# Rows of w_out in runs of four, and every fourth column of w_in as weights

## The chip, the cores and the metric

The kernel runs on one core of one Trainium2 chip. The core has five engines that run side by side: TensorE (matmuls; its weight loads are listed apart), VectorE, ScalarE, GpSimd and SyncE, called PE, PEld, DVE, ACT, POOL and SP in the profile. Transfers between the chip's main memory and the on-chip memory are issued by SP, ACT or POOL and carried by 16 DMA engines that all of them share. The metric is the device time of one execution in microseconds (us), lower is better, given as the median of several runs.

## What is computed

Two layers are fused. The first is attention with a sliding window of 128 tokens and a bias that falls off linearly with distance, over 8 batches, 8 heads, 576 tokens and 64 columns a head. The second is a dense layer pair with a hard-swish between: its input is the attention's output, taken as 4608 tokens of 512 columns. Cut to what matters:

```python
# q, k, v: (8, 8, 576, 64); w_in: (512, 2048); w_out: (2048, 512)
scores = q @ k.T / sqrt(64) - slope[head] * abs(i - j)     # kept where 0 <= i - j < 128
attn = softmax(scores) @ v
x = attn.transpose(0, 2, 1, 3).reshape(4608, 512)
h = x @ w_in
g = h * clip(h + 3, 0, 6) / 6
out = g @ w_out
```

The column of `h` that a row of `w_out` is multiplied with has the same index, from 0 to 2047. How the 2048 indices are divided among partitions and tiles is free, as long as both weights do it alike.

## The kernel before

Tokens are worked through in tiles. The attention of a batch is done head pair by head pair (32 pairs in all, `g` in the code), and its output is transposed into `xT`, a ring of 2304 tokens (`RING`, line 50) with the 512 model columns on the partitions in four slices. The dense pair goes over nine tiles of 512 tokens (`NT`).

For a token tile, `moe_up` (line 462) makes 16 blocks of 128 columns of `h`. Block `ms` takes four matmuls (`up_mms`, line 444), one for each slice `ks` of the model columns: the weights are a 128x128 piece of `w_in_sb`, the moving operand is 512 columns of `xT`. The fifth token tile reaches past the end of the ring, and there each matmul is cut into two of 256 columns, each with a weight load of its own (lines 445 to 449). ScalarE takes a clipped form of the block out of the accumulator (line 470) and VectorE multiplies it with the block itself, to bf16 in `gbuf` (line 471): partition `p` of block `ms` holds one column of `h` for all 512 tokens.

`moe_down` (line 488) takes 128 tokens at a time and accumulates 16 matmuls, one for each `ms`, whose weights are a piece of `gbuf` and whose moving operand is `w_out_sb[:, ms, :]`, 512 columns (line 501). The sums are copied out (line 510) and stored. The last 128 tokens have a routine of their own (`last_rows`, line 474).

The order of the work is written out by hand, for every engine and queue (`manual_schedule`, line 716). The strings in `ORDER` (line 513) interleave up blocks (U) and quarters of down steps (D), and `fill` (line 523) puts them between the steps of attention. An engine carries out its instructions in the order in which the code issues them.

The weights come in through POOL's queue, since these transfers turn float32 into bf16 on their way. `load_w_in(g)` (line 164) loads 512 columns of `w_in`. `load_w_out(g)` (line 169) loads 512 rows of `w_out` into four blocks of `w_out_sb`: row `g*512 + m*128 + p` goes to partition `p`, block `4*g + m`, so each row of 512 values is a run of its own. The four calls stand in `second_batch` (line 632), after POOL's casts of v of batch 1 and ahead of its mask for head pair 7 (line 354, written to `gbuf`) and its casts of k and q of batch 2 (line 227). Ahead of this time `w_out_sb` serves as room for the attention of batch 0 (`rooms`, line 281), so that matmuls of lines 383 and 391 also read it.

On SP's queue, `load_tokens(2, "v")` (lines 108 to 113, five transfers of rows of 256 bytes) follows at line 639, behind a small POOL write at line 638, then the k and q loads of batch 3 (lines 98 and 112). POOL casts v of batch 2 into `vbuf` (lines 187 and 190) and the matmuls of attention (lines 383 and 391) read that.

Of the kernel before, what the change touches and what calls it, by code (L numbers as in the profile page):

```python
# [18 lines left out]
def kernel(  # L19
# [9 lines left out]
    nc = tc.nc  # L29
# [23 lines left out]
    xT = perm.tile([128, n_ks, RING + SP - S], BF16)  # L53
    w_in_sb = perm.tile([128, n_ks, d_ff], BF16)
    w_out_sb = perm.tile([128, n_ms, d_model], BF16)
    ident = perm.tile([128, 128], BF16)
    bias3 = perm.tile([128, 1], FP32)
    warm = perm.tile([128, 1], FP32)
# [111 lines left out]
    def load_w_out(g):  # L170
        nc.gpsimd.dma_start(  # L171
            out=w_out_sb[:, ts(g, 4), :],
            in_=moe_w_out[ds(g * 512, 512), :].rearrange("(m p) d -> p m d", p=128))

    def second_w_in():
        nc.gpsimd.memset(w_out_sb[:, 4, 0:1], 0.0)
# [267 lines left out]
    def up_mms(nt, ms, k0, k1, hps):  # L444
        at0 = nt * NT % RING
        n = min(NT, RING - at0)
        for lo, hi, src in ((0, n, at0), (n, NT, 0)):
            if lo == hi:
                continue
            for ks in range(k0, k1):  # L450
                nc.tensor.matmul(hps[:, lo:hi], lhsT=w_in_sb[:, ks, ts(ms, 128)],  # L451
                                 rhs=xT[:, ks, ds(src, hi - lo)],
                                 start=(ks == 0), stop=(ks == n_ks - 1))

    def up_begin(nt, ms, n):
        hps = ps_h.tile([128, NT], FP32, tag="h", name="hps")
        up_mms(nt, ms, 0, n, hps)
        begun[nt, ms] = hps, n
# [3 lines left out]
    def moe_up(nt, ms):  # L462
        gts[nt] = gbuf[nt % 2]
        hps, n = begun.pop((nt, ms), (None, 0))
        if hps is None:
            tag = UP_BANKS.get(ms, "h") if nt == 0 else "h"
            hps = BANKS[tag].tile([128, NT], FP32, tag=tag, name="hps")
        up_mms(nt, ms, n, n_ks, hps)
        r6 = rpool.tile([128, NT], FP32, tag="r6", name="r6")
        nc.scalar.activation(out=r6, in_=hps, func=ACT.Relu, bias=bias3[:, 0:1], scale=1.0 / 6.0)  # L470
        nc.vector.scalar_tensor_tensor(out=gts[nt][:, ms, :], in0=r6, scalar=1.0, in1=hps,  # L471
                                       op0=ALU.min, op1=ALU.mult)
# [145 lines left out]
    def second_batch():  # L618
# [12 lines left out]
        for i in range(4):  # L631
            load_w_out(i)
# [131 lines left out]
```

## Time and profile before

| what | value |
|---|---|
| median of 3 runs | 322.76 us (322.67 to 324.89) |
| profiled execution | 323.3 us, of which the span is 321.6 us |
| granted TensorE clock | 0.998 |
| up matmuls, line 451 | 640 of them, 144.8 us busy |
| down matmuls, line 501 | 560 of them, 137.8 us busy |
| w_out transfers, line 171 | 4 of 512 KB, 7.9 to 15.6 us from issue to landing |
| w_in transfers, line 166 | 4 of 512 KB, 6.3 to 9.5 us from issue to landing |

The span runs from the first to the last instruction of one profiled execution. A line of a group gives the code line, the engine, the operation, what it writes and reads, how many there are; then their busy time in us, the mean length of one in ns, and the idle time of the engine just before them with what ended it. A line of the chain or the timeline gives the start in us, the length in us, and what ran. A line of a stretch gives its length and then, for each engine, its busy time in the order PE, PEld, DVE, ACT, POOL, followed by the clock, the share of the DMA engines and the GB/s. Records of matmuls and of weight loads overlap, so the length of one record is longer than the pace at which they follow one another.

### The profile page before, as it was taken

The numbers are of one execution on the slowest core, as the hardware profiler recorded it, in microseconds if no ns is written. First come the engines' busy times: TensorE is split into PE (matmuls) and PEld (weight loads), VectorE is DVE, ScalarE is ACT, GpSimd is POOL, SyncE is SP. The second block draws the span as 40 slices with busy tenths as digits, with TensorE's granted clock in tenths as the row PEclk, the third lists the DMA queues.
The fourth block names the chain that finished last, engine by engine and source line by source line (L and its number), as shares of the span: only waits on it lengthen the run. The fifth ranks groups of instructions, "written<-read, shape, count | busy, mean of one in ns | idle before, by whom it ended". The sixth has DMA issues, their size and how long they took to land.

```text
span 321.6 us, 7050 instructions
## 1 busy us (share of the span) xinstructions
PE 312.4 (97%) x2738; PEld 167.6 (52%) x2738; DVE 173.0 (54%) x338; ACT 195.6 (61%) x334; POOL 141.1 (44%) x249
## 2 busy tenths in 40 slices
PE   7889999999999999999999999999999999999996
PEld 5565465455555554554667654554554444444443
DVE  6667674554456555555555555555655455455510
ACT  3758976877767766766676667666764344244401
POOL 8455493594493767366745665463331000000000
PEclk9999999999999999999999999999999999999999
DMA  7999999899999999999999989922112200000112
GB/s 276 202 333 208 247 270 196 210 258 194 212 248 166 244 201 203 193 229 199 192 199 202 237 173 212 214 72 86 23 53 66 75 34 35 33 33 33 67 53 77
DMA packets 131425, 51.90 MB, mean 161 GB/s; under 512 B 118976, under 2 KB 123328, under 8 KB 131392
## 3 DMA queue, kind: packets, MB, share of 16 engines
q1 hardware_dynamic: 126160, 45.36, 66.2%
q0 software_dynamic: 4224, 4.19, 8.2%
q10 hardware_dynamic: 1008, 1.90, 1.6%
q8 instruction: 21, 0.34, 0.5%
q14 instruction: 12, 0.10, 0.1%
HBM read 36.70 MB, written 9.44 MB: 143 GB/s over the span
## 4 chain that ended last, share of the span: by engine, by line
PE 82%; DMA 10%; SPq 2%; POOL 2%; DVE 1%; ACT 1%; issue 1%; POOLq 0%
PE ops L501 37%; PE hps L451 33%; DMA w_out_sb<-in_moe_w_out_dram 5%; DMA ldbuf<-in_v_dram 3%; PE scd L296 3%; DMA ldbuf<-in_k_dram 2%; PE av L391 2%; SPq L112 2%; PE av L383 2%; PE sco L328 1%; PE ops L482 1%; PE w L153 1%; POOL w_out_sb L171 1%; PE tp L219 0%; ACT kTb L244 0%
## 5 line engine op out<-in xcount | busy, mean ns | idle before, releaser
L471 DVE SCALAR_TENSOR_TENSOR gbuf<-r,hps 128x512 bf16<-128x512 f32 x144 | 98.7, 687 | 102.5 <-ACT r L470 100.2
L470 ACT ACTIVATE r<-hps,bias 128x512 f32<-128x512 f32 x144 | 98.9, 689 | 88.9 <-PE hps L451 88.7
L451 PE MATMUL hps<-xT,w_in_sb 128*128 128x512 bf16 (+1 forms) x640 | 144.8, 358 | 0.5 <-ACT xT L438 0.3
L501 PE MATMUL ops<-w_out_sb,gbuf 128*128 128x512 bf16 x560 | 137.8, 379 | 0.3 <-DMA w_out_sb<-in_moe_w_out_dram 0.3
L451 PEld LDWEIGHTS <-w_in_sb 128*128 128x128 bf16 x640 | 59.2, 98 | 54.8 <-issue 0.8
L501 PEld LDWEIGHTS <-gbuf 128*128 128x128 bf16 x560 | 51.8, 98 | 56.7 <-issue 0.6
L354 POOL TENSOR_SCALAR_AFFINE_SELECT pd<-pd 128x512 bf16<-128x512 bf16 x48 | 29.7, 634 | 34.5 <-ACT pd L351 34.5
L364 POOL TENSOR_SCALAR_AFFINE_SELECT po<-po 128x512 bf16<-128x512 bf16 x48 | 30.3, 636 | 32.5 <-ACT po L361 32.3
L351 ACT ACTIVATE pd<-scd,bias_d 128x512 bf16<-128x512 f32 x48 | 31.7, 685 | 4.7 <-PE scd L296 4.7
L510 DVE COPY osb<-ops 128x512 f32<-128x512 f32 x33 | 22.7, 687 | 20.4 <-PE ops L501 20.2
L361 ACT ACTIVATE po<-sco,bias_o 128x512 bf16<-128x512 f32 x48 | 33.0, 688 | 0.0
L194 POOL CAST tbuf<-ldbuf 128x512 bf16<-128x512 f32 (+1 forms) x45 | 25.6, 614 | 16.7 <-DMA qTb<-tbuf 9.0
L402 DVE TENSOR_TENSOR avs<-av,rc 128x384 bf16<-128x384 f32 (+1 forms) x48 | 23.6, 491 | 1.6
L391 PEld LDWEIGHTS <-pd 128*128 128x128 bf16 x192 | 14.3, 97 | 8.3 <-issue 0.5
L383 PE MATMUL av<-vbuf,po 128*128 128x65 bf16 x192 | 18.0, 193 | 0.0
L391 PE MATMUL av<-vbuf,pd 128*128 128x65 bf16 x192 | 17.3, 194 | 0.3 <-ACT kTb L244 0.3
L187 POOL CAST vbuf<-ldbuf 128x1024 bf16<-128x1024 f32 x14 | 14.3, 1044 | 4.3 <-DMA ldbuf<-in_v_dram 4.3
L383 PEld LDWEIGHTS <-po 128*128 128x128 bf16 x192 | 14.3, 98 | 2.9 <-DVE avs L402 0.5
L367 ACT ACTIVATE p4buf<-sco,bias_d 128x64 bf16<-128x64 f32 x48 | 15.5, 324 | 0.0
L227 POOL CAST pr<-ldbuf 128x576 bf16<-128x576 f32 x20 | 12.9, 670 | 5.0 <-DMA ldbuf<-in_k_dram 3.1
L296 PE MATMUL scd<-qTb,kTb 64*128 64x128 bf16 x256 | 12.7, 219 | 1.7 <-DVE kTb L220 0.9
L296 PEld LDWEIGHTS <-kTb 64*128 64x128 bf16 x256 | 7.2, 94 | 13.4 <-issue 9.7
(96 smaller groups left out, 217.4 us busy)
## 6 DMA issues: line engine op xcount, KB each, us to landing
out_dram<-osb SPq DMA_DIRECT2D x33, 256.0 KB, 2.4
ldbuf<-in_v_dram SPq DMA_DIRECT2D x32, 256.0 KB, 5.6
ldbuf<-in_q_dram SPq DMA_DIRECT2D x20, 256.0 KB, 4.9
ldbuf<-in_k_dram SPq DMA_DIRECT2D x16, 256.0 KB, 4.5
ldbuf<-in_q_dram SPq DMA_DIRECT2D x12, 288.0 KB, 7.3
ldbuf<-in_k_dram SPq DMA_DIRECT2D x12, 288.0 KB, 7.6
w_in_sb<-in_moe_w_in_dram POOLq DMA_DIRECT2D x4, 512.0 KB, 8.8
w_out_sb<-in_moe_w_out_dram POOLq DMA_DIRECT2D x4, 512.0 KB, 11.6
```

Source lines behind the costliest of these rows:

```text
L194: nc.gpsimd.tensor_copy(out=tbuf[:m, :, j, :], in_=s[:m, j, :, :].rearrange("p (i e) d -> p i (e d)", e=2))
L296: nc.tensor.matmul(scd[:, e, ts(j, 128)], lhsT=kT[r, j, :], rhs=qT[r, j, :], start=first, stop=first or j == 3)
L351: nc.scalar.activation(out=pd[:, e, :, :].rearrange("p j c -> p (j c)"), in_=sc[:, e, :], func=ACT.Exp, bias=bias_d[:, h:h + 1], scale=scale)
L354: nc.gpsimd.affine_select(out=pd[:, e, :, :], in_=pd[:, e, :, :], pattern=[[0, 4], [1, 128]], channel_multiplier=-1, base=0, compare_op=AL ...
L361: nc.scalar.activation(out=po[:, e, :, :].rearrange("p j c -> p (j c)"), in_=sc[:, e, :], func=ACT.Exp, bias=bias_o[:, h:h + 1], scale=scale)
L364: nc.gpsimd.affine_select(out=po[:, e, :, :], in_=po[:, e, :, :], pattern=[[0, 4], [-1, 128]], channel_multiplier=1, base=-1, compare_op=A ...
L383: nc.tensor.matmul(out_av, lhsT=po[:, e, qt % 4, :], rhs=vb[:, qt - 1, h, :], start=True, stop=False)
L391: nc.tensor.matmul(out_av, lhsT=d, rhs=vb[:, qt, h, :], start=(qt == 0), stop=True)
L451: nc.tensor.matmul(hps[:, lo:hi], lhsT=w_in_sb[:, ks, ts(ms, 128)], rhs=xT[:, ks, ds(src, hi - lo)], start=(ks == 0), stop=(ks == n_ks - 1))
L470: nc.scalar.activation(out=r6, in_=hps, func=ACT.Relu, bias=bias3[:, 0:1], scale=1.0 / 6.0)
L471: nc.vector.scalar_tensor_tensor(out=gts[nt][:, ms, :], in0=r6, scalar=1.0, in1=hps, op0=ALU.min, op1=ALU.mult)
L501: nc.tensor.matmul(ops[nt, sub], lhsT=gts[nt][:, ms, ts(sub, 128)], rhs=w_out_sb[:, ms, :], start=(ms == 0), stop=(ms == n_ms - 1))
```

## The change

The w_out transfer takes its 512 rows in another order. Row `g*512 + p*4 + m` now goes to partition `p`, block `4*g + m`: a partition gets four neighbouring rows, 8 KB of float32 in one run, into 4 KB of its own that also lie together. To match, block `ms` of the up step must hold the columns `(ms // 4)*512 + 4*p + ms % 4` of `h`. A view of `w_in_sb` with the columns divided by four gives them: the weights of an up matmul are 128 columns that lie four apart, 8 bytes in bf16. The loads of w_in, the number and order of all instructions, and the down matmuls are as before.

```diff
@@ -53,6 +53,7 @@
     w_in_sb = perm.tile([128, n_ks, d_ff], BF16)
     w_out_sb = perm.tile([128, n_ms, d_model], BF16)
+    w_in_cols = w_in_sb.rearrange("p k (g c m) -> p k g m c", g=4, m=4)
@@ -170,7 +171,7 @@
     def load_w_out(g):
         nc.gpsimd.dma_start(
             out=w_out_sb[:, ts(g, 4), :],
-            in_=moe_w_out[ds(g * 512, 512), :].rearrange("(m p) d -> p m d", p=128))
+            in_=moe_w_out[ds(g * 512, 512), :].rearrange("(p m) d -> p m d", p=128))
@@ -448,7 +449,7 @@
             for ks in range(k0, k1):
-                nc.tensor.matmul(hps[:, lo:hi], lhsT=w_in_sb[:, ks, ts(ms, 128)],
+                nc.tensor.matmul(hps[:, lo:hi], lhsT=w_in_cols[:, ks, ms // 4, ms % 4, :],
                                  rhs=xT[:, ks, ds(src, hi - lo)],
                                  start=(ks == 0), stop=(ks == n_ks - 1))
```

## The prediction

> **What bounds the kernel now.** I read the page first (busy shares, then the chain that ended last, then the costliest groups), then the waits of TensorE, then the stretch from 41 to 60 us, in which w_out is loaded, and last the pace of single matmuls in the timeline and the chain.
>
> ```profile
> span 321.6 us, 7050 instructions
> PE 312.4 (97%) x2738; PEld 167.6 (52%) x2738; DVE 173.0 (54%) x338; ACT 195.6 (61%) x334; POOL 141.1 (44%) x249
> ...
> PE 82%; DMA 10%; SPq 2%; POOL 2%; DVE 1%; ACT 1%; issue 1%; POOLq 0%
> ...
> L451 PE MATMUL hps<-xT,w_in_sb 128*128 128x512 bf16 (+1 forms) x640 | 144.8, 358 | 0.5 <-ACT xT L438 0.3
> ...
> L451 PEld LDWEIGHTS <-w_in_sb 128*128 128x128 bf16 x640 | 59.2, 98 | 54.8 <-issue 0.8
> ```
>
> TensorE is the bound: it works in 312.4 of 321.6 us. The chain's "DMA 10%" is misleading. A chain passes through whatever released a step, however short the wait was. Half of that 10% is the w_out transfer, and the next three answers (the chain, TensorE's waits, the busy time of the stretch) show what it really costs:
>
> ```profile
> 43.46 15.55 DMA w_out_sb<-in_moe_w_out_dram
> 59.05 1.02 PE ops L501 x4
> ...
> PE ops L501 <- DMA w_out_sb<-in_moe_w_out_dram: 0.3, 1, 0.3
> ...
> 41.00:60.00 19.00, 18.05 (x193) 10.49 (x191) 11.22 (x20) 14.65 (x25) 11.26 (x19) 1.00 1.09 214
> ```
>
> The last quarter of w_out lands 15.55 us after its issue, but TensorE waits for it only once, for 0.33 us (the timeline has the matmuls of line 501 at 59.05 with 0.33 us of idle before them). In the whole stretch TensorE is idle for 19.00 - 18.05 = 0.95 us.
>
> Whether the other half of the change costs anything depends on how long one weight load may take before a matmul waits for it. The chain gives the pace of matmuls that follow one another, each with its own weight load:
>
> ```profile
> 156.80 0.03 PE av L383
> 156.83 0.03 PE av L391
> 156.86 0.03 PE av L383
> 156.89 0.03 PE av L391
> 156.92 1.75 PE hps L451 x16
> 158.66 0.86 PE ops L501 x4
> ```
>
> A matmul with 512 columns takes 0.86/4 = 216 ns. One with 256 columns takes 1.75/16 = 109 ns. The narrow ones of attention (65 columns) follow one another every 30 ns, and each of them loads 128x128 weights of its own. So a contiguous load occupies the load path for at most 30 ns, although its record shows 98 ns: the records overlap.
>
> **The change, part by part.** The sum is made against the profiled execution, 323.3 us, of which 321.6 us are span and 1.7 us lie around it. It stands 0.5 us above the median, 322.76 us.
>
> *1. The four w_out transfers have other rows.* Nothing is moved: four issues at the same places in POOL's order and the same bytes. In the DMA packet records each load is now 512 packets, 32 for each of 16 engines, of 1024 B written (2048 B read); four neighbouring rows make 128 packets, 8 an engine, of 8192 B read. The records give a packet's price by its size. Beside 22 ns for 256 B (between 40 and 60 us) stand 108 ns for 2304 B, thus some 11 ns plus 0.042 ns a byte, and w_out's own packets fit at 96 ns undisturbed. A packet of 8192 B would take 11 + 344 = 355 ns in place of 4 x 96 = 384, so an engine is done with its 32 rows 32 x 29 = 0.9 us sooner. While v of batch 2 shares the engines (52 to 55 us), the records alternate one to one (154 packets of w_out and 155 of v in a us), so fewer, larger packets also give w_out more of each engine. From below the gain is nothing, if the packets are cut as before. From above it is 0.33 us, since TensorE waits no longer than that; with a knock-on it cannot pass the 0.95 us of idle in the stretch. I take 0.33 us, because 0.9 us sooner is more than that. The first three quarters land ahead of their use already: issue to landing takes 7.9 us at the least against a first use 10.5 us after the issue (41.23 to 51.71), and TensorE shows no other wait for them.
>
> *2. The loads behind it.* What w_out gains in share, v of batch 2 on SP's queue loses while both are under way. SP issues that load from 47.95 to 59.90 us, one issue of it taking 6.29 us, and the k and q loads of batch 3 follow on the same queue. Up to 56 us v got 750 of its 4608 packets; afterwards it moves 985 in a us. Held back entirely, it would have 750/985 = 0.8 us more to move after w_out, which is 0.9 us earlier: as much as before. The reader behind it is POOL's cast (line 187, done at 63.6 us, which waits for v for 0.6 us), and behind that the matmuls of attention at 64.53 us. They have 0.9 us in hand, so 0 is the price, and at most 0.8 us would be lost if w_out were no quicker and that reserve were gone.
>
> *3. POOL's issues.* Each takes 0.76 us (3.0 us for four). With a quarter of the runs it may be shorter; SP's issues differ little by runs (0.53 us for 128 of 2304 B, 0.70 for 1024 of 256 B). So it is between no change and 3.0 us less. What stands behind on POOL is the mask on gbuf at 44.20 to 45.46 us, read by the matmuls at 47.02 us. With 1.5 us in hand there is nothing to gain: 0.
>
> *4. The weights of line 451 are every fourth column, 8 bytes apart.* There are 640 loads, 512 under matmuls of 216 ns and 128 under matmuls of 109 ns (the token tile that wraps round the ring). If such a load occupies the path for L ns, the cost is 512 x (L - 216) + 128 x (L - 109), each counted only where it is above zero. No row shows a strided weight load, so I bound it. From below: 30 ns as now, costing 0; no gain is possible, since the loads are covered already. The nearest rate on TensorE itself is that of the moving operand, one column at a time: 128 columns in 216/4 = 54 ns, costing 0. At half that rate it is 107 ns, costing 0 by a hair. At a quarter it is 214 ns: 128 x 105 = 13.4 us. From above, four times the whole record: 4 x 98 = 392 ns, or 512 x 176 + 128 x 283 = 126 us. I take 0, by the two nearest things in the trace. One is the 54 ns, at which TensorE is seen to take in columns one after another from the same memory. The other is far, ScalarE reading with a long step:
>
> ```profile
> 46.93 0.63 ACT L438 COPY xT<-tb 128x576 bf16<-128x576 bf16 x1
> 47.45 0.77 ACT L244 COPY kTb<-tp 128x640 bf16<-128x640 bf16 x1
> ```
>
> The first reads its columns in order, the second every 128th column: 1.09 and 1.20 ns an element, so the step costs a tenth and not a factor. The cover of 216 and 109 ns is 3.6 times the present load even in the tight form.
>
> [...]
>
> Sum: 323.3 - 0.33 + 0 + 0 + 0 = 323.0 us for the profiled execution, and 322.76 - 0.33 = **322.4 us** for the median.
>
> **The rivals.**
> *Slower: strided weights no longer fit under the matmul.* Place: line 451. It decides from L = 109 ns, first in the tile with matmuls of 256 columns, and is worth 1% (3.2 us) from L = 134 ns. At a quarter of the streaming rate, 214 ns, the time is 322.8 + 13.4 = 336.2 us. Above 216 ns every up matmul waits, and 392 ns would give 322.8 + 126 = 449 us. For it: no row shows such a load, and TensorE has 3% of idle in all, so anything uncovered shows in full. Against it: the cover, 3.6 and 7 times the present load. Also against it: the 128 weights are spread over four times the bytes, and if the load had to pass over them all at its present pace it would take 4 x 30 = 120 ns, which costs 128 x 11 = 1.4 us and gives 324.2 us, still within 1%.
> *No effect: w_out comes no sooner, or the wait returns.* Either the packets are cut as before, or the slowest engine still sets the landing. For it: the records of completion for the last load run from 55.6 to 57.3 us for fifteen engines and to 58.7 us for one, so one late engine holds back the whole. Time: 322.8 us.
> *Faster by more than 1%.* That needs 3.2 us; the stretch in which the transfer matters has 0.95 us of idle, so 321.8 us is the floor of this mechanism. Only a wait elsewhere that moves by chance could do more.
>
> **How the numbers follow.** The smallest difference that a measurement of this kernel can tell from no change is about 1%. The forecast (loads covered, 0.33 us gained) has 0.52; no effect 0.19; pitch between 109 and 216 ns 0.13, of which 0.03 stays under 1%; pitch above 216 ns 0.14; faster by over 1% 0.02. So within 1% is 0.52 + 0.19 + 0.03 = 0.74, slower 0.10 + 0.14 = 0.24, faster 0.02. The range reaches from 321.6 us (the floor of 321.8, less the spread of 0.1 us between median and lowest run) to 336.2 us (a quarter of the rate). It leaves out 0.14 + 0.02 = 0.16. The likeliest case's own range is 321.6 to 323.5 us.
>
> **What would show it.** The L451 weight loads should still last about 98 ns, or up to twice that, with the up matmuls at 216 and 109 ns. The software queue should have some 1500 packets fewer (4 x 384), the last w_out transfer should land before 58.7 us, and TensorE's wait for it should be gone. POOL's cast of v should end by 64.5 us. I am wrong if the chain shows L451 at more than 0.86 us for four, if TensorE's busy time grows, or if a wait for v appears ahead of the matmuls at 64.5 us.

## The result and the profile after

The changed kernel takes 344.06 us (median of 4 runs, 341.66 to 347.94) against 323.07 us before (median of 4): a ratio of 1.0613, with a 95% interval of 1.0539 to 1.0687. It is 6% slower. The ratio compares the means of the faster executions, without the one of 347.94 us. Its profiled execution took 341.66 us, with a span of 340.0 us, 18.4 us more than the profiled execution before. The forecast of 322.4 us and the whole range missed it.

The page of the changed kernel, beside the one of before (the code lines have moved by one, so line 451 is now 452 and 501 is 502):

```profile
span 340.0 us, 7011 instructions
PE 311.8 (92%) x2699; PEld 178.3 (52%) x2738; DVE 173.7 (51%) x338; ACT 196.0 (58%) x334; POOL 139.8 (41%) x249
...
PE   7853199999999999999999999999999999999996
...
PEclk9997589999999999999999999999999999999999
...
L452 PE MATMUL hps<-xT,w_in_sb 128*128 128x512 bf16 (+1 forms) x623 | 144.6, 361 | 17.2 <-DMA w_in_sb<-in_moe_w_in_dram 16.0
```

TensorE's busy time is about what it was, 311.8 us against 312.4 (some matmul records are missing from this trace, 2699 of 2738, so it reads a little low). So the matmuls did not become slower by anything like 18 us, and there is no sign of weight loads that hold them up. What grew is idle time, and nearly all of it lies in three slices of the PE row, between 17 and 43 us. The group of up matmuls says what ended it: a transfer of **w_in**, which the change does not touch. TensorE's waits say how much (us in total, times, the longest), and the timeline of its weight loads (start in us, length, operation, idle before it) shows the place:

```profile
PE hps L452 <- DMA w_in_sb<-in_moe_w_in_dram: 16.0, 2, 10.5
```

```profile
22.27 0.11 PEld L452 LDWEIGHTS <-w_in_sb 128*128 128x128 bf16 x1
27.97 0.14 PEld L452 LDWEIGHTS <-w_in_sb 128*128 128x128 bf16 x2 [5.59 <-DMA w_in_sb<-in_moe_w_in_dram]
...
30.20 0.15 PEld L452 LDWEIGHTS <-w_in_sb 128*128 128x128 bf16 x1
41.38 0.14 PEld L452 LDWEIGHTS <-w_in_sb 128*128 128x128 bf16 x2 [11.03 <-issue]
```

The first block of the first token tile loads its weights for slice 0 of the model columns at 22.27 us, as early as before. Its second load, slice 1, waits until 27.97 us: until the second w_in transfer has landed, whose columns it does not read. The second block does the same. Slice 0 goes at 30.20 us, and slice 1 waits until 41.38 us, when the third and fourth transfers are in. Before the change these loads followed one another without a gap:

```profile
21.94 0.37 PEld L451 LDWEIGHTS <-w_in_sb 128*128 128x128 bf16 x3
```

The waiting goes the other way as well. In the code the third and fourth w_in loads (lines 607 and 608 of the kernel before) stand behind three matmuls of the first block (line 603) and ahead of the second block's (line 612). This fits that it is the second block that waits for them. And POOL now holds these two loads back until the three matmuls are done, though they write none of the columns that those read. Before, and after the change (in brackets the idle time of POOL and what ended it):

```profile
27.83 1.48 POOL L166 DMA_DIRECT2D w_in_sb<-in_moe_w_in_dram  x2
```

```profile
29.32 1.48 POOL L167 DMA_DIRECT2D w_in_sb<-in_moe_w_in_dram  x2 [2.23 <-PE hps L452]
```

So the transfers for which the second block waits also start 1.5 us later.

From this the 18.4 us can be added up. From the first up load to the first down matmul it was 51.71 - 21.94 = 29.8 us and is 70.5 - 22.27 = 48.2 us, 18.4 us more. From there to the end of the span it was 269.9 us and is 269.5. So the whole loss lies ahead of the first down matmul: 16.0 us are the two waits, and 2.4 us are left. The row PEclk points to those. The granted clock falls to 0.7 and 0.5 in the last two idle slices; its mean is 0.76 from 20 to 41 us and 0.91 from 41 to 60 us. By finer stretches it is 1.00 from 22.3 to 27.2 us, 0.50 from 27.4 to 30.7, 1.00 from 30.8 to 34.1, 0.50 from 34.3 to 44.3 and 1.00 from 44.5 to 60. TensorE's timeline shows what the matmuls after each wait then take, and the chain, in the last two lines, has the landing that ends the second wait and nine transposes at the full clock:

```profile
27.98 1.04 PE L452 MATMUL hps<-xT,w_in_sb 128*128 128x512 bf16 x2 [5.49 <-DMA w_in_sb<-in_moe_w_in_dram]
28.82 0.74 PE L433 MATMUL tb<-ident,avs 128*128 128x128 bf16 x5
29.35 1.17 PE L255 MATMUL tp<-ident,pr 128*128 128x128 bf16 x9
30.31 0.59 PE L452 MATMUL hps<-xT,w_in_sb 128*128 128x512 bf16 x1
41.41 1.44 PE L452 MATMUL hps<-xT,w_in_sb 128*128 128x512 bf16 x3 [10.51 <-DMA w_in_sb<-in_moe_w_in_dram]
42.64 1.16 PE L255 MATMUL tp<-ident,pr 128*128 128x128 bf16 x9
43.60 1.64 PE L452 MATMUL hps<-xT,w_in_sb 128*128 128x512 bf16 x5
45.07 0.67 PE L255 MATMUL tp<-ident,pr 128*128 128x128 bf16 x9
...
30.05 11.22 DMA w_in_sb<-in_moe_w_in_dram
...
45.24 0.50 PE tp L255 x9
```

The starts give the pace. From 27.98 to 30.31 us run two up matmuls and fourteen transposes, 2.33 us, where 216 ns for an up matmul and 0.50/9 = 56 ns for a transpose would make 1.2. From 41.41 to 45.07 us run eight up matmuls and nine transposes, 3.66 us in place of 2.2. Together that is 2.5 us more, about what was left. What ran slowly between the two waits cost little by itself, since TensorE would otherwise have waited there longer; the 1.4 us behind the second wait could not be hidden. The stretches agree with this: the clock stands at half from some 5 us into the first wait of 5.5 us, again from some 3.3 us into the second of 10.5 us, and in full from about 3 us after the second. What sets the clock is not shown here. The median of the runs lies further off, 21.0 us above. The waits differ from execution to execution (17.6 us in the profiles of two experiments below), which may be why.

### The profile page after: what moved, and what is told of

Same layout as the page of the kernel before. It is cut to its first block, busy times and chain, and to the rows that moved or that the text cites. A ratio compares the mean times of both kernels' runs of the same rounds, so it can differ in the third digit from the quotient of the medians.

```text
span 340.0 us, 7011 instructions
## 1 busy us (share of the span) xinstructions
PE 311.8 (92%) x2699; PEld 178.3 (52%) x2738; DVE 173.7 (51%) x338; ACT 196.0 (58%) x334; POOL 139.8 (41%) x249
## 2 busy tenths in 40 slices
DMA packets 129889, 51.90 MB, mean 153 GB/s; under 512 B 118976, under 2 KB 121280, under 8 KB 129856
## 4 chain that ended last, share of the span: by engine, by line
PE 83%; DMA 7%; ACT 4%; DVE 3%; issue 2%; POOL 0%; SPq 0%; POOLq 0%
PE hps L452 35%; PE ops L502 34%; DMA w_in_sb<-in_moe_w_in_dram 6%; PE scd L297 3%; PE av L392 2%; PE av L384 2%; ACT r L471 1%; PE sco L329 1%; DMA out_dram<-osb 1%; PE ops L483 1%; PE w L154 1%; ACT kTb L245 1%; PE sco L308 1%; PE tp L220 1%; DVE kTb L221 1%
## 5 line engine op out<-in xcount | busy, mean ns | idle before, releaser
L502 PE MATMUL ops<-w_out_sb,gbuf 128*128 128x512 bf16 x538 | 133.8, 379 | 2.6 <-issue 2.1
L452 PEld LDWEIGHTS <-w_in_sb 128*128 128x128 bf16 x640 | 68.6, 114 | 64.6 <-issue 12.6
L352 ACT ACTIVATE pd<-scd,bias_d 128x512 bf16<-128x512 f32 x48 | 31.7, 684 | 4.7 <-PE scd L297 4.7
L297 PE MATMUL scd<-qTb,kTb 64*128 64x128 bf16 x256 | 12.7, 219 | 1.7 <-DVE kTb L221 0.9
```

Of the source, the lines that this page charges most:

```text
L297: nc.tensor.matmul(scd[:, e, ts(j, 128)], lhsT=kT[r, j, :], rhs=qT[r, j, :], start=first, stop=first or j == 3)
L352: nc.scalar.activation(out=pd[:, e, :, :].rearrange("p j c -> p (j c)"), in_=sc[:, e, :], func=ACT.Exp, bias=bias_d[:, h:h + 1], scale=scale)
L452: nc.tensor.matmul(hps[:, lo:hi], lhsT=w_in_cols[:, ks, ms // 4, ms % 4, :], rhs=xT[:, ks, ds(src, hi - lo)], start=(ks == 0), stop=(ks == ...
L502: nc.tensor.matmul(ops[nt, sub], lhsT=gts[nt][:, ms, ts(sub, 128)], rhs=w_out_sb[:, ms, :], start=(ms == 0), stop=(ms == n_ms - 1))
```

## The experiments

**Theory.** The build is taken to make a matmul wait for a transfer when what the one reads and the other writes seem to overlap. A w_in transfer writes four stretches of 512 columns in each partition, 2048 columns apart. A contiguous piece of 128 columns falls between them and is seen as apart. A piece of every fourth column seems to be compared by outer bounds instead: of the 8192 places in a partition the second transfer reaches from 512 to 7167, and slices 1 to 3 of the first group lie inside that. Slice 0 lies below it, which fits the loads that did not wait. By the same bounds the third and fourth transfers overlap what the first block reads, which fits POOL's wait. *Rival 1*: strided weights load too slowly. *Rival 2*: the w_out transfer, or its place on POOL, does it.

**The change with unbroken transfers.** `w_in_sb` is laid out by load group, so that a transfer writes one stretch; the weights stay as strided as before. (The code shows only what matters; `...` stands for the rest of a statement.)

```diff
-    w_in_sb = perm.tile([128, n_ks, d_ff], BF16)
+    w_in_sb = perm.tile([128, 4, n_ks, 512], BF16)
-    w_in_cols = w_in_sb.rearrange("p k (g c m) -> p k g m c", g=4, m=4)
+    w_in_cols = w_in_sb.rearrange("p g k (c m) -> p g k m c", m=4)
-            out=w_in_sb[:, :, ts(g, 512)],
+            out=w_in_sb[:, g, :, :],
-    ... lhsT=w_in_cols[:, ks, ms // 4, ms % 4, :], ...
+    ... lhsT=w_in_cols[:, ms // 4, ks, ms % 4, :], ...
```

> The whole change, with w_in_sb laid out by load group, [128, 4, 4, 512] in place of [128, 4, 2048], so that what one w_in transfer writes is one unbroken stretch per partition. Theory (the first up matmuls wait for w_in transfers whose columns they do not read, because a strided operand and a transfer that writes four separate stretches are compared by their outer bounds): the bounds no longer overlap, the two waits of 5.5 and 10.5 us go, and the time is 322.0 to 324.0 us, with weight loads still at about 113 ns. Rival 1 (weights with a step load too slowly for the matmuls to cover): still 340 us or more, as the loads are as strided as before. Rival 2 (the transfer of w_out or its place on POOL does it): still 340 us or more.

Measured: 324.11 us against 323.85 (ratio 1.0011, interval 0.9988 to 1.0035). The loss is gone with every strided load and the new w_out transfer in place, so both rivals fall. POOL no longer waits for TensorE ahead of a w_in load either. Its page, its group of weight loads, and the up matmuls of 256 columns in its chain:

```profile
span 321.6 us, 7050 instructions
PE 312.8 (97%) x2738; PEld 177.1 (55%) x2738; DVE 173.3 (54%) x338; ACT 195.4 (61%) x334; POOL 139.6 (43%) x249
```

```profile
L452 PEld LDWEIGHTS <-w_in_sb 128*128 128x128 bf16 x640 | 68.4, 114 | 47.8 <-issue 0.7 <-DMA w_in_sb<-in_moe_w_in_dram 0.3
```

```profile
156.83 1.75 PE hps L452 x16
158.58 0.86 PE ops L502 x4
```

The record of a load is 114 ns in place of 98, and the matmuls above them still take 1.75/16 = 109 ns.

**The layout alone**, a control: the same two layout edits in the kernel before, with contiguous weights.

> The kernel before, with w_in_sb laid out by load group and nothing else. A control for the layout itself: all theories expect 322.0 to 324.0 us. What separates it from the run with layout and change together is the pure price or gain of the change without its wait; by the forecast 0.3 us.

Measured: 323.89 us against 323.85 (1.0008, 0.999 to 1.0026). The layout itself is worth nothing that can be measured. Nor is the change beside it: 324.11 us with it, 323.89 without.

**Each part alone.** First only the w_out edit, then only the weights, each in the old layout and shown against the kernel before:

```diff
-    in_=moe_w_out[ds(g * 512, 512), :].rearrange("(m p) d -> p m d", p=128))
+    in_=moe_w_out[ds(g * 512, 512), :].rearrange("(p m) d -> p m d", p=128))
```

> Only w_out is loaded with four neighbouring rows per partition; the up matmuls keep their contiguous columns, so the output is that of other pairings of rows and columns. Theory: no wait on w_in, 322.0 to 323.5 us, with TensorE's 0.33 us wait for w_out gone and the last w_out transfer landing about 1 us or more sooner. Rival 2 (the w_out transfer does it): 340 us or more. Rival 1: as the theory.

Measured: 323.79 us against 323.85 (0.999, 0.9974 to 1.0006). The last w_out transfer lands 12.2 us after its issue in place of 15.6.

```diff
-    ... lhsT=w_in_sb[:, ks, ts(ms, 128)], ...
+    ... lhsT=w_in_cols[:, ks, ms // 4, ms % 4, :], ...
```

> Only the weights of the up matmuls are every fourth column; w_out is loaded as before, so the output is that of other pairings. Theory: both waits for w_in stand, 340 to 348 us, as in the whole change. Rival 1: the same time, but with up matmuls more than 216 and 109 ns apart. Rival 2: 322 to 324 us.

Measured: 344.36 us against 323.85 (1.0643, 1.061 to 1.0677), the whole loss, with this line among TensorE's waits, and 2.5 us in which POOL waits for TensorE ahead of a w_in load:

```profile
PE hps L452 <- DMA w_in_sb<-in_moe_w_in_dram: 17.6, 2, 11.3
```

**The first token tile alone, and the others alone.** If the wait is the cause, only the tile during which w_in still arrives matters.

```diff
+    ... lhsT=w_in_cols[:, ks, ms // 4, ms % 4, :] if nt == 0 else w_in_sb[:, ks, ts(ms, 128)], ...
```

> The whole change in the old layout, but the up matmuls read every fourth column only for the first token tile; the eight later tiles read contiguous columns, so their output is that of other pairings. Theory (all the loss is the wait for w_in transfers at the first up blocks): the whole loss stands, 340 to 348 us. Rival 1 (each strided weight load costs): the loss falls to about a ninth, 325 to 327 us.

Measured: 344.03 us against 323.5 (1.0671, 1.0605 to 1.0736), with 17.6 us of waits for w_in: the whole loss from the strided loads of one token tile in nine. The reverse exchanges the two operands:

> The reverse: the first token tile reads contiguous columns (its output is that of other pairings), the eight later ones every fourth column, in the old layout. Theory: no transfer of w_in is under way any more when strided columns are read, so 322.5 to 324.5 us, as before. Rival 1: about eight ninths of the loss, 341 us.

Measured: 323.8 us against 323.5 (1.0009, 0.9992 to 1.0026): the strided loads of the other eight tiles cost nothing that can be measured.

**The old layout with smaller transfers.** Each w_in transfer is cut into its four slices, so that none reaches over another.

```diff
+        for k in range(n_ks):
+            nc.gpsimd.dma_start(
+                out=w_in_sb[:, k, ts(g, 512)],
+                in_=moe_w_in[ds(k * 128, 128), ts(g, 512)])
```

> The whole change in the old layout, but each w_in transfer cut into four, one for each slice of the model columns, so that each writes one unbroken stretch and none reaches over another's. Theory (outer bounds of a transfer that writes four stretches): the waits of 16 us go and the time falls to 323 to 328 us; the upper end allows for twelve more issues on POOL, 0.5 us or so each. Rival (any strided operand waits for all transfers into its tile): 340 us or more.

Measured: 326.57 us against 324.11 (1.0106, 1.004 to 1.0173). TensorE's waits for w_in fall from 16.0 to 1.5 us, and POOL's timeline shows the issues:

```profile
PE hps L453 <- DMA w_in_sb<-in_moe_w_in_dram: 1.5, 3, 0.8
```

```profile
12.34 2.27 POOL L168 DMA_DIRECT2D w_in_sb<-in_moe_w_in_dram  x4
```

So the operand may be strided and the layout may be the old one, if the transfer writes one stretch. The remaining 2.5 us are put down to the sixteen issues, though no run shows their price alone. Four of them take POOL 2.27 us, where the single one took 0.89, and the last of w_in lands at 43.1 us in place of 38.0.

**How long a load occupies the path.** In the third and fourth token tiles each up matmul is cut into eight of 64 columns, each with its own load, first in the kernel before, then in the change with unbroken transfers.

```diff
+            step = 64 if nt in (2, 3) else hi - lo
+            for c in range(lo, hi, step):
+                for ks in range(k0, k1):
+                    nc.tensor.matmul(hps[:, ds(c, step)], lhsT=w_in_sb[:, ks, ts(ms, 128)],
+                                     rhs=xT[:, ks, ds(src + c - lo, step)], ...
```

> The kernel before, with each up matmul of the third and fourth token tiles cut into eight of 64 columns, each with its own weight load: the pace then shows how long a contiguous load occupies the path. Expected: about 30 ns from one to the next (27 ns of columns), some 0.9 us for 32 of them in place of four of 216 ns.

> The same cut in the kernel with the whole change and w_in_sb laid out by load group. Theory: a strided load occupies the path longer than a contiguous one but less than 109 ns; its record is 15 ns longer (113 against 98 ns), so 30 to 60 ns from one narrow matmul to the next, 45 taken; at 109 ns or more the rival of slow loads would have been near. If the pace is still 30 ns, the 15 ns are delay alone and no rate.

Two more runs take the first of these and read every eighth, then every sixteenth column from the second token tile on (`w_in_sb` viewed with 8 or 16 columns to a step).

> The kernel before with the narrow up matmuls of 64 columns in the third and fourth token tiles, and from the second token tile on weights that are every eighth column (16 bytes apart), so that its output is that of other pairings. It measures how the pace of loads goes with the step: 29 ns contiguous and 33 ns at 8 bytes are measured. [...]

> The same with every sixteenth column (32 bytes apart). [...]

From the chains of the four kernels, in the order contiguous, every fourth, eighth and sixteenth column:

```profile
102.22 0.93 PE hps L453 x32
```

```profile
107.09 1.06 PE hps L454 x32
```

```profile
106.34 1.90 PE hps L454 x32
```

```profile
103.78 1.96 PE hps L454 x32
```

A load and its 64 columns take 29, 33, 59 and 61 ns. The times of these kernels, one run each, are 326.46, 329.70, 358.11 and 360.72 us, and the 1024 narrow matmuls account for the differences: 1024 x 30 ns = 31 us of the 31.7 between the first and the third. The full matmuls stay at their pace in all four, here with every sixteenth column:

```profile
193.62 1.78 PE hps L454 x16
...
198.28 0.87 PE hps L454 x8
```

That is 109 to 111 ns for 256 columns. The 45 ns expected for every fourth column were too high.

## Why the prediction was wrong

**What bounds the kernel** was read rightly: TensorE with 3% of idle, so that any new wait shows in full. It did.

**Step 1, w_out.** The direction was right, the sum was not. The kernel moves 129889 packets in place of 131425, 1536 fewer. A packet of 8192 B read takes some 324 ns by the packet records (the median of 512 in the profile of the changed kernel), against 355 forecast. (The prices of 22 and 108 ns are means from 30 to 60 us; between 40 and 60 us they are 21 and 98.) The 29 ns are saved once for each packet of four rows, so an engine's 32 rows of one load save 8 x 29 ns = 0.2 us, and 0.9 us is what all four loads save together. In the kernel with unbroken transfers the last w_out transfer lands 12.7 us after its issue in place of 15.6, and TensorE's wait for it is gone. But that wait is also missing in the control with the old w_out transfer, which lands 14.6 us after its issue: there the first down matmul came at 52.3 us in place of 51.7, late enough by itself. So the 0.33 us belonged to one profile of the kernel before, and nothing of it can be seen in the time: the intervals are 0.9988 to 1.0035, and 0.9974 to 1.0006 with the w_out edit alone.

**Step 2, the loads behind it**, and **step 3, POOL's issues**: no new wait for v appeared, and the four issues shortened from 0.76 to 0.55 us each, at no gain, as forecast.

**Step 4, the weights.** With L at 33 ns, against the 54 taken, the formula gives 0, and with the waits out of the way the time is that of before: the rate costs nothing. The step that failed is the sentence around it, "If such a load occupies the path for L ns, the cost is ...". It priced the new operand by its rate alone. It took for granted, without a word on it, that the operand's waits stay the same; each block does still read columns of its own transfer only. The runs showed in its place 16.0 us of waits for three transfers that the blocks do not read, and some 2.5 us that TensorE's work took longer at a lower clock (0.50 from 27.98 to 30.31 us, 0.59 from 41.41 to 45.07). The rival on the slower side had the right line and the wrong mechanism, and its chance of 0.24 was for something that did not happen. (The lower end of the range is 321.7 us by its own terms, 321.8 - 0.1, and not 321.6.)

The price could have been read before. The first up load stood at 21.94 us, and the POOL rows had the second w_in issue at 18.70 and the last two at 27.83 us, each landing 6.3 to 9.5 us later. Three of four transfers were thus still to land when the first block began, and everything hung on its needing only the first. And two of them were still to be issued, behind matmuls for which they could be made to wait.

One thing is argued and not shown: that the build compares outer bounds. The loads that waited and the ones that did not, POOL's wait for the first block's matmuls, the vanished waits with either form of unbroken transfer, and the untouched later tiles all fit it, but no run shows the comparison itself.

There is no version that beats the kernel before: the change with unbroken transfers is equal to it within 0.35%.

## What to carry to other kernels

When an operand's shape in memory changes, ask two questions: how fast it is read, and which writes it will now be held to overlap with; look up which transfers into the same buffer are still under way at its first use, and which are issued after it. A buffer laid out so that each transfer writes one unbroken stretch kept those waits exact here, at no cost. A stall on the bounding engine cost more than its length here, since the clock was lower after it, 0.50 behind the first wait and 0.59 behind the second: beside 16.0 us of waits the work took some 2.5 us longer, 1.4 of them behind the second wait.

## What the runs showed of the hardware

Weight loads of 128 columns, each with a matmul of 64 columns, follow one another every 29 ns contiguous, every 33 ns with weights 8 bytes apart, every 59 ns at 16 bytes and every 61 ns at 32. So the pace does not go with the distance passed over: from 8 to 16 bytes it rises by 26 ns, from 16 to 32 by 2 ns. Why the rise lies there is not shown, and steps beyond 32 bytes were not run. Up to a step of 32 bytes the load still fits under a matmul of 256 columns (109 to 111 ns). The record of a load is longer than its pace, 98 and 116 ns in the first two of these runs (means), 161 and 162 ns in the others (medians), so it does not say how long the load path is occupied.
